# The second convolution's hand-written tile order is replaced, and its last inverse tile is split over two PSUM tiles

## The chip, the cores and the metric

The kernel runs on one core of a Trainium2 chip. The metric is the device time of one execution in microseconds (us), taken as the median of several runs. A profiled execution of the kernel before gives a trace: which instruction ran when on which engine. TensorE (PE in the profile) multiplies matrices and writes to PSUM; VectorE (DVE) and ScalarE (ACT) move results out of PSUM; SyncE (SP) issues the DMAs.

## The reference, cut to what matters

The program computes four layers on a sequence of 2048 rows with 512 channels: attention layer A, convolution layer B, then A and B again with the same weights. Each layer is preceded by a layer norm and added to its input. The change concerns only the last layer, the second B. With `u` the normalized input and `K` the convolution kernel of 2048 taps per channel, it computes

```python
Kf = rfft2(Kp)                 # K padded to 4096
Uf = rfft2(up)                 # u padded to 4096
Yf = Uf * Kf
y = irfft2(Yf)[..., :L]        # back to 2048 rows
y = y.T + u * Dskip            # the skip is folded into K before its transform
x = x + y                      # what is written out
```

## The kernel before

The convolution is done as a Fourier transform in two stages, a product, and an inverse transform in two stages, all stages as matmuls. It is class `FftB`. The channels are treated in two groups of 256 (`g` = 0 and 1), and every stage of a group is cut into 8 tiles (the last stage into 4). Each tile fills one PSUM tile `pb` of 128 x 1024 floats, which one engine then takes out of PSUM. The stages are named by one letter in an order string, which `run` walks through:

- `U` (function `f1`): first forward stage. 16 matmuls (line 756), then an eviction to `a1s` (line 745) by DVE (`UD`) or ACT (`UA`).
- `u` (function `u_f2`): second forward stage. 16 matmuls (line 763), then an eviction to `ub` by ACT (line 818). It reads all of `a1s` of its group, so the first `u` of a group needs all eight `U` evictions of it.
- `m` (function `u_mult`): product with the kernel's transform. Two DVE multiplications (line 805), into `t1` and `t2`. After each, `pump` issues three loads for a later piece of the kernel's transform on SP (lines 795 and 797), into a ring of ten.
- `y` (function `i1`): first inverse stage. 16 matmuls (lines 831 and 832), eviction to `z` (line 745) by DVE (`yD`) or ACT (`yA`). The profile names the destination `xnT` for group 0 and `z` for group 1, since group 0 reuses an older buffer. It reads all of `t1` and `t2` of its group, so the first `y` of a group needs all eight `m` of it.
- `zgt` (function `i2`): second inverse stage, tile `t` of group `g`; each tile covers four row blocks `a`. `D` means 8 matmuls (lines 847 and 848) and a DVE addition to the residual `x_sb` (line 851). `A` means four more matmuls that add the residual on PE (line 846) and a copy by ACT (line 853). `B` ("both") gives two row blocks to DVE and two to ACT. It reads all of `z` of its group. Right after each tile `store` writes it out by a DMA on SP (line 1434).

In what follows a tile is named by its letter, group and number: y13 is tile 3 of the first inverse stage of group 1. Tiles of `U`, `u`, `m` and `y` are taken in the order 00 to 07, then 10 to 17; `z` tiles carry their numbers in the order string.

The order string is written out by hand, and no scheduler moves anything: every engine executes its instructions in the string's order. What couples the engines, beside the data, is room. `ptile` deals out four PSUM tiles in rotation, so PE can start a tile only after the tile four before it has been evicted. There are three buffers for `ub`, so ACT can evict a `u` tile only after the `m` three before it is done.

PSUM tiles are tracked as a whole. In the last tile, `z13B`, DVE and ACT take halves of the same PSUM tile, and the ACT copy is made to wait for the DVE addition. The two halves are stored by two DMAs of 128 KB; all other tiles by one of 256 KB.

Of the kernel before, what the change touches and what calls it, by code (L numbers as in the profile page):

```python
# [11 lines left out]
ALU = mybir.AluOpType  # L12
# [8 lines left out]
P = 128  # L21
# [17 lines left out]
DQG = 64  # L39
# [20 lines left out]
T3 E31D x1 E30A P20 P22  # L60
"""
ORDER1 = """
UD UA UA UD UA UA UD UA UD UA UD u UD u m UA u u m UA m u u UA m UD m
u u m m m u u m u m m u u m u m m u yA yA yA m u yA yA yA yA
m yD yA yD yD yA z00D yD yA z01D yA yA z02D z03D z10D z11D z12A z13B
"""

def build_a_consts(tc, nc, cpool, tpool):
# [617 lines left out]
def build_g2(nc, tmp, p21, g2_dram, room):  # L686

    s8 = 2.0 * math.pi / 65536 * SIN_SHRINK
    own = tmp.tile([P, 2, 8 * P], I32, name="g2_i")
    gi = [own[:, 0], own[:, 1], *(room[:, (2 + h) * 16 * P:(3 + h) * 16 * P].bitcast(I32) for h in range(2))]  # L690

    def indices(h):
        for k, bias in enumerate((16384.0, 32768.0)):
            g = gi[h][:, k * 4 * P:(k + 1) * 4 * P]
            nc.gpsimd.iota(g.rearrange("p (a m) -> p a m", m=P), pattern=[[8, 4], [128, P]], base=32 * h, channel_multiplier=0)
            nc.gpsimd.tensor_scalar(g, g, p21, bias, ALU.mult, ALU.add)

    def sines(h):
        gs = room[:, h * 8 * P:(h + 1) * 8 * P]
        nc.scalar.activation(gs, low16(gi[h]), ACT.Sin, scale=s8)  # L700
        nc.sync.dma_start(g2_dram[:, :, h * 4:(h + 1) * 4, :], gs.rearrange("p (k a m) -> p k a m", k=2, a=4))

    return indices, sines


class FftB:
# [129 lines left out]
    def i2(self, g, t, eng):  # L836

        nc, x_sb = self.nc, self.x_sb
        z = self.S[g]["z"]
        dsl = slice(g * DQG * 4, (g + 1) * DQG * 4)  # L840
        p4 = self.ptile([P, 4, DQG * 4])
        n_add = {"dve": 4, "both": 2, "act": 0}[eng]
        for j in range(4):
            a = t * 4 + j
            if j >= n_add:
                nc.tensor.matmul(p4[:, j, :], lhsT=self.ident[:], rhs=x_sb[:, a, dsl], start=True, stop=False)
            nc.tensor.matmul(p4[:, j, :], lhsT=self.g2[:, 0, a, :], rhs=z[:, a, :], start=(j < n_add), stop=False)
            nc.tensor.matmul(p4[:, j, :], lhsT=self.g2[:, 1, a, :], rhs=z[:, NA + a, :], start=False, stop=True)
        if n_add:
            xr = x_sb[:, t * 4:t * 4 + n_add, dsl]  # L850
            nc.vector.tensor_tensor(xr, p4[:, 0:n_add], xr, ALU.add)
        if n_add < 4:
            nc.scalar.copy(x_sb[:, t * 4 + n_add:t * 4 + 4, dsl], p4[:, n_add:4])

    def run(self, order, u, done=lambda g, t: None, k=None, late=(), more={}):
        late, cnt = list(late), self.cnt
# [419 lines left out]
def kernel(  # L1276
# [16 lines left out]
    nc = tc.nc  # L1293
# [18 lines left out]
    u = xnT[:].rearrange("p t (b r) -> p (t b) r", r=64).rearrange("p q (a r) -> p q a r", r=4)  # L1312
# [7 lines left out]
    x_sb = xpool.tile([P, NA, D], BF16, name="x_sb")  # L1320
# [30 lines left out]
    with tc.tile_pool(name="ctmp_g2", bufs=1) as g2tmp, tc.manual_schedule(engines=MAN):  # L1351
        gx, gs = build_g2(nc, g2tmp, C["p21"], g2_dram, kp[:].rearrange("p q a r -> p (q a r)"))
# [24 lines left out]
    with tc.manual_schedule(engines=MAN):  # L1377
# [21 lines left out]
        def last(*ops):  # L1399
            def f():  # L1400
                for op, *ix in ops:
# [6 lines left out]
                     e=lambda ft: la.front_ext(3, "dve", ft))  # L1408
# [18 lines left out]
    with tc.manual_schedule(engines=MAN):  # L1427
        out_v = out.rearrange("b (p a) d -> p (b a) d", p=P)

        def store(g, t):  # L1430
            gs = slice(g * 4 * DQG, (g + 1) * 4 * DQG)
            n = 2 if (g, t) == (1, 3) else 4
            for a in range(t * 4, t * 4 + 4, n):
                nc.sync.dma_start(out_v[:, a:a + n, gs], x_sb[:, a:a + n, gs])

        fb.run(ORDER1, u, store)
    fb.c_mid.close()
# [33 lines left out]
```

## Time and profile before

| what | value |
|---|---|
| median of 4 runs | 429.02 us (428.54 to 429.66) |
| the profiled execution's own time | 429.06 us |
| its span in the trace | 427.2 us |
| granted TensorE clock over the span | 0.99 of full speed |
| DVE busy | 394.8 us, 92% of the span |
| PE busy | 353.9 us, 83% |
| ACT busy | 323.2 us, 76% |
| second convolution, first matmul to last eviction | 375.8 to 422.9 us |

The span is the time from the first to the last record of the trace; the execution's own time is 1.8 us longer. In a line of the timeline or of the chain the first number is the start in us from the beginning of the span and the second a duration in us; a bracket at the end names how long the engine had been idle before, and on whom it waited. In the table by stretch each engine has its busy time and the number of its instructions, PEclk is the TensorE clock granted (1.00 is full speed), and DMA the mean busy share of the 16 DMA engines.

### The profile page before, as it was taken

The page shows a single profiled execution, that of the slowest core. Times are in us where ns is not written, and L with a number is a line of the kernel's source. Part 1 is how long each engine was busy: PE and PEld are TensorE (multiplying, and loading weights), DVE is VectorE, ACT ScalarE, POOL GpSimd, SP SyncE. Part 2 cuts the span into 40 slices and gives each one's busy share as a digit, 9 for nine tenths or more (in the row PEclk, how much of TensorE's full clock was granted, in tenths as well). Part 3 has the DMA queues.
Part 4 walks back from the last instruction along what each step waited for, and adds up shares of the span by engine and source line. Part 5 has one row for each costly group of instructions (what it writes and reads, how often), then busy time and mean ns, then how long its engine had stood idle before and what let it go on. Part 6 is the DMA issues. An engine that isn't in the chain of part 4 may idle for free.

```text
span 427.2 us, 12737 instructions
## 1 busy us (share of the span) xinstructions
PE 353.9 (83%) x5506; PEld 264.9 (62%) x5506; DVE 394.8 (92%) x537; ACT 323.2 (76%) x554; POOL 43.9 (10%) x46
## 2 busy tenths in 40 slices
PE   3000169999999899999998899999999999997894
PEld 2000127667765687767887898555566777776793
DVE  8999999999999999996999949899999999889864
ACT  6999999986455389887999978855556568689961
POOL 3000300000598000001300000000000020000000
PEclk9999998999999899999999999999999999999999
DMA  7930732132116743572245591820141055416315
GB/s 218 392 104 12 82 78 69 33 69 58 26 41 188 243 111 99 168 308 102 77 170 188 218 329 38 258 69 2 30 111 35 2 226 219 150 52 181 118 40 161
DMA packets 62466, 54.16 MB, mean 127 GB/s; under 512 B 33893, under 2 KB 50890, under 8 KB 61130
## 3 DMA queue, kind: packets, MB, share of 16 engines
q1 hardware_dynamic: 62266, 53.22, 41.0%
q8 instruction: 43, 0.70, 0.7%
q10 hardware_dynamic: 144, 0.13, 0.1%
q14 instruction: 13, 0.11, 0.1%
HBM read 30.28 MB, written 13.24 MB: 102 GB/s over the span
## 4 chain that ended last, share of the span: by engine, by line
PE 47%; DVE 19%; ACT 10%; DMA 4%; issue 3%; SPq 2%; DVEq 0%; ACTq 0%
PE po L412 9%; DVE pav L404 5%; DVE prod L295 4%; PE pq L351 4%; PE pk L1165 4%; PE pq L424 4%; PE pp L1103 4%; PE L L302 3%; PE pp L242 3%; PE pq L185 2%; DVE t L805 2%; PE pb L831 2%; PE pb L832 2%; DVE a1s L745 2%; ACT a1s L745 2%
## 5 line engine op out<-in xcount | busy, mean ns | idle before, releaser
L404 DVE TENSOR_TENSOR pav<-attn,v_ext 128x4096 bf16<-128x4096 bf16 x32 | 73.0, 2284 | 0.3 <-DMA v_ext<-v_ext 0.3
L412 PEld LDWEIGHTS <-pav 128*128 128x128 bf16 x1024 | 59.9, 99 | 11.1 <-DVE pav L404 7.5
L295 DVE TENSOR_TENSOR prod<-qT,kT_ext 128x4096 bf16<-128x4096 bf16 x29 | 66.4, 2310 | 0.2
L412 PE MATMUL po<-ident,pav 128*128 128x128 bf16 x1024 | 63.9, 222 | 3.1 <-DVE pav L404 2.8
L1093 PE MATMUL pt<-ident,x_blk 128*128 128x128 bf16 x64 | 6.5, 252 | 43.1 <-ACT x_blk L158 43.1
L1005 DVE TENSOR_TENSOR A_t<-A_t,pow_t 128x1024 bf16<-128x1024 bf16 (+4 forms) x46 | 38.4, 879 | 0.2
L1093 PEld LDWEIGHTS <-x_blk 128*128 128x128 bf16 x64 | 5.3, 115 | 46.0 <-ACT x_blk L158 44.0
L818 ACT CAST ub<-pb 128x1024 bf16<-128x1024 f32 x32 | 32.4, 1059 | 1.3 <-DVE t L805 1.1
L353 ACT CAST v_ext<-pq 128x512 bf16<-128x512 f32 x32 | 18.8, 586 | 19.3 <-PE pq L351 18.1
L424 PE MATMUL pq<-wop,oT 128*128 128x512 bf16 x128 | 32.9, 379 | 0.0
L302 PEld LDWEIGHTS <-prod 128*128 128x128 bf16 x928 | 27.1, 96 | 8.9 <-DVE prod L295 3.2
L415 ACT CAST oT<-po 128x512 bf16<-128x512 f32 x32 | 18.6, 580 | 18.1 <-PE po L412 18.0
L1103 PE MATMUL pp<-xnT,kT_ext 128*128 128x512 bf16 x96 | 27.8, 421 | 4.7 <-ACT qT L1108 2.7
L831 PE MATMUL pb<-Wp,t 128*128 128x128 bf16 x256 | 30.2, 219 | 1.8 <-ACT ub L818 1.2
L763 PE MATMUL pb<-a1s,w_sb 128*128 128x64 bf16 x768 | 27.7, 193 | 4.8 <-ACT ub L818 3.5
L832 PE MATMUL pb<-WpJ,t 128*128 128x128 bf16 x256 | 30.0, 219 | 1.0 <-DVE t L805 1.0
L351 PE MATMUL pq<-wv,xnT 128*128 128x512 bf16 x128 | 30.7, 379 | 0.0
L745 DVE CAST a1s<-pb 128x1024 bf16<-128x1024 f32 x22 | 26.2, 1220 | 4.9 <-PE pb L756 4.8
L763 PEld LDWEIGHTS <-w_sb 128*128 128x128 bf16 x768 | 24.8, 98 | 7.5 <-issue 5.9
L302 PE MATMUL L<-ind,prod 128*128 128x8 bf16 x928 | 27.4, 166 | 1.3 <-DVE prod L295 1.1
L832 PEld LDWEIGHTS <-t 128*128 128x128 bf16 x256 | 24.9, 98 | 3.6 <-DVE t L805 1.8
L745 ACT CAST a1s<-pb 128x1024 bf16<-128x1024 f32 x26 | 25.6, 1041 | 2.0 <-PE pb L756 2.0
(227 smaller groups left out, 862.0 us busy)
## 6 DMA issues: line engine op xcount, KB each, us to landing
w_sb<-w_dram SPq DMA_DIRECT2D x8, 1024.0 KB, 7.3
w_dram<-w_zero SPq DMA_DIRECT2D x1, 4096.0 KB, 15.4
kf_ring<-kf_dram SPq DMA_DIRECT2D x13, 256.0 KB, 3.6
kf_ring<-kf_dram SPq DMA_DIRECT2D x26, 128.0 KB, 3.6
v_ext<-v_ext SPq DMA_DIRECT2D x4, 784.0 KB, 6.3
x_blk<-in_A_x_dram SPq DMA_DIRECT2D x4, 512.0 KB, 4.4
kT_ext<-in_A_wqkv_dram SPq DMA_DIRECT2D x4, 512.0 KB, 9.3
x_sb<-in_A_x_dram SPq DMA_DIRECT2D x4, 512.0 KB, 4.8
```

What stands on the lines that cost most here:

```text
L295: nc.vector.tensor_tensor(pr, self.qT[q][:, ft].unsqueeze(1).to_broadcast([P, W, 4, P]), kap, ALU.mult)
L302: self.nc.tensor.matmul(L[:, al, w, ft * 8:(ft + 1) * 8], lhsT=pr[:, w, al, :], rhs=self.c["ind8"][:], start=(ft == 0 and w == 0 and al % ...
L351: nc.tensor.matmul(pp[:], lhsT=xnT[:, dt, a * P:(a + 1) * P], rhs=wv[:, dt, :], start=(dt == 0), stop=(dt == NDT - 1))
L404: nc.vector.tensor_tensor(pv[:], attn[:, n % 4].unsqueeze(2).to_broadcast([P, W, DH, H]), vap, ALU.mult)
L412: nc.tensor.matmul(po[:, ft, :], lhsT=pvf[:, w, ft * P:(ft + 1) * P], rhs=ident[:], start=(w == 0 and ft == 0), stop=(w == W - 1), skip_gr ...
L424: nc.tensor.matmul(pw[:], lhsT=oT[:, ftp, :], rhs=self.wo[:, ftp, :], start=False, stop=(ftp == NDT - 1))
L745: (self.nc.scalar.copy if eng == "act" else self.nc.vector.tensor_copy)(dst, src)
L763: nc.tensor.matmul(p2[:, j, :], lhsT=self.w2[:, ec * EC + j, :], rhs=a1s[:, ec * EC + j, :], start=True, stop=True)
L831: nc.tensor.matmul(p3[:, j, :], lhsT=t1[:, dql, :], rhs=wp_r, start=True, stop=False)
L832: nc.tensor.matmul(p3[:, j, :], lhsT=t2[:, dql, :], rhs=wpj_r, start=False, stop=True)
L1005: return lambda: nc.vector.tensor_tensor(*args)
L1103: nc.tensor.matmul(pps[kind, b, ft][:], lhsT=la.wqk[:, dt, c:c + P], rhs=la.xnT[:, dt, b * 512:(b + 1) * 512], start=(dt == 0), stop=(dt = ...
```

## The change

The order string of the second convolution is replaced. The numbers of tiles are the same, and so is the work on PE. One `U` and one `y` tile more are evicted by DVE (8 and 5 in place of 7 and 4) and one of each fewer by ACT (8 and 11 in place of 9 and 12). The ACT tile of the last stage is `z11` in place of `z12`. The last tile, `z13B`, is made of two PSUM tiles of 128 x 512 floats, each with two row blocks: one is added by DVE, the other copied by ACT, and neither waits for the other. Its result is stored by one DMA of 256 KB, so that there are eight stores in place of nine. On all engines everything ahead of the second convolution is the same instructions in the same order.

```diff
 ORDER1 = """
-UD UA UA UD UA UA UD UA UD UA UD u UD u m UA u u m UA m u u UA m UD m
-u u m m m u u m u m m u u m u m m u yA yA yA m u yA yA yA yA
-m yD yA yD yD yA z00D yD yA z01D yA yA z02D z03D z10D z11D z12A z13B
+UD UA UD UA UD UA UD UA UD UA UD u UD u u m UA u m UD UA m u m u m
+u m UA m u m u m u m u u yD yA u m yA m m u u u m yA m yA
+yA m yD yD yA yD yA yA yA yD z01D z03D yA yA z00D z02D z12D z11A z10D z13B
 """
...
-        p4 = self.ptile([P, 4, DQG * 4])
-        n_add = {"dve": 4, "both": 2, "act": 0}[eng]
-        for j in range(4):
-            a = t * 4 + j
+        if eng == "both":
+            for h, e in enumerate(("dve", "act")):
+                self.i2_rows(z, t * 4 + 2 * h, 2, dsl, e)
+        else:
+            self.i2_rows(z, t * 4, 4, dsl, eng)
+
+    def i2_rows(self, z, a0, n, dsl, eng):
+
+        nc, x_sb = self.nc, self.x_sb
+        p4 = self.ptile([P, n, DQG * 4])
+        n_add = n if eng == "dve" else 0
+        for j in range(n):
+            a = a0 + j
...
-            xr = x_sb[:, t * 4:t * 4 + n_add, dsl]
-            nc.vector.tensor_tensor(xr, p4[:, 0:n_add], xr, ALU.add)
-        if n_add < 4:
-            nc.scalar.copy(x_sb[:, t * 4 + n_add:t * 4 + 4, dsl], p4[:, n_add:4])
+            xr = x_sb[:, a0:a0 + n, dsl]
+            nc.vector.tensor_tensor(xr, p4[:], xr, ALU.add)
+        else:
+            nc.scalar.copy(x_sb[:, a0:a0 + n, dsl], p4[:])
...
-            n = 2 if (g, t) == (1, 3) else 4
-            for a in range(t * 4, t * 4 + 4, n):
-                nc.sync.dma_start(out_v[:, a:a + n, gs], x_sb[:, a:a + n, gs])
+            ts = slice(t * 4, t * 4 + 4)
+            nc.sync.dma_start(out_v[:, ts, gs], x_sb[:, ts, gs])
```

## The prediction

> **What bounds the kernel now.** Only the second convolution changes, so I first asked the table by stretch which engine is full there.
>
> ```profile
> 380.00:384.00 4.00, 3.72 (x112) 3.24 (x107) 4.00 (x4) 3.87 (x5) 0.00 (x0) 1.00 0.02 4
> 384.00:388.00 4.00, 3.52 (x100) 3.12 (x97) 4.00 (x8) 4.00 (x5) 0.00 (x0) 1.00 0.28 69
> 402.00:406.00 4.00, 4.00 (x72) 4.00 (x72) 2.75 (x5) 4.00 (x5) 0.00 (x0) 1.00 0.00 0
> 406.00:410.00 4.00, 4.00 (x74) 4.00 (x72) 2.70 (x3) 3.21 (x4) 0.00 (x0) 1.00 0.02 4
> 414.00:418.00 4.00, 4.00 (x53) 3.74 (x51) 2.56 (x3) 1.93 (x3) 0.00 (x0) 1.00 0.32 92
> ```
>
> The columns are PE, PE's weight loads, DVE, ACT, POOL, clock, DMA share, GB/s. Up to 402 us DVE is full and PE is not; from 402 us on PE is full and DVE has about 1.3 us free in every 4. So there are two regimes. Where the second begins is seen in the timelines of ACT and DVE:
>
> ```profile
> 400.86 2.85 ACT L745 CAST xnT<-pb 128x1024 bf16<-128x1024 f32 x3
> 403.57 1.06 ACT L818 CAST ub<-pb 128x1024 bf16<-128x1024 f32 x1
> 404.48 3.82 ACT L745 CAST xnT<-pb 128x1024 bf16<-128x1024 f32 x4
> 404.66 1.29 DVE L805 TENSOR_TENSOR t<-ub,kf_ring 128x1024 bf16<-128x1024 bf16 x2 [1.21 <-ACT ub L818]
> 406.69 1.23 DVE L745 CAST xnT<-pb 128x1024 bf16<-128x1024 f32 x1 [0.73 <-PE pb L832]
> ```
>
> Between 400.86 and 408.3 us ACT evicts y00 to y06 and, after y02, the last `ub` (u17) one behind the other, a start every 0.91 us. DVE, with the last product m17 still to do, idles 1.21 us until u17 is out. PE is held by ACT too: y10 starts at 406.51, 0.05 us after ACT has emptied the PSUM tile four back (y04), and y11 and y12 likewise. From y13 on PE runs without a wait: y tiles every 0.89 us, `zD` tiles every 0.87.
>
> The end is read from the chain and the waits:
>
> ```profile
> 421.40 0.12 PE pb L848
> 421.55 0.70 DVE x_sb L851
> 422.27 0.59 ACT x_sb L853
> ACT x_sb L853 <- DVE x_sb L851: 0.8, 1, 0.8
> ```
>
> The ACT half of z13 waits for the DVE half. But computing is not all of the end:
>
> ```profile
> DMA  0007999189982999739999999999940000000000
> L1434 SPq DMA_DIRECT2D out_dram<-x_sb x9: 372/389/529, 412.5 to 422.9; - x9
> DMA to landing us min/median/max: 2.3/2.3/2.8
> ```
>
> The first line cuts 418 to 427.3 us into 40 slices: from about 422 to 425 us the DMA engines are full without a break. In the trace the last stores are issued at 421.17 (z11), 421.63 (z12), 422.27 and 422.88 (z13), and land at 423.52, 424.33, 424.81 and 425.31. Alone, 256 KB land 2.3 us after issue; in a queue each lands 0.82 us after the one before. So the end was fixed by the queue that z11's store opened: 423.52 + 0.81 + 0.98 = 425.31. The span ends 1.93 us after it.
>
> **The change part by part.** *Nothing before 375.8 us moves*; the instructions are the same.
>
> *DVE up to m17.* In the new order DVE has nine evictions before m17's end (eight `U`, and y00, which stands ahead of m12) and sixteen product pairs. Two evictions in a row start 1.14 us apart in the trace (U10, U12: 380.73, 381.87), pairs 1.205 (m11 to m13: 396.14, 397.34, 398.54). DVE starts its first eviction at 376.49 as before. If it never waits, m17 ends at 376.49 + 9 x 1.14 + 16 x 1.205 + 0.09 (the pipelined end) = 406.12. Does it wait? I carried the new order through tile by tile: each step starts at the latest of its engine being free, its operands, and its PSUM tile four back. Durations are those of the rows: 16 matmuls take 0.42 us for `U`, 0.44 for `u`, 0.84 for `y`; the eviction starts 0.26 after the last matmul's start; ACT takes 1.02, one every 0.91. The tightest places: `U` evictions on DVE have their matmuls done 0.35 us early; m07 has its `ub` 0.6 early, m10 0.9; y00 is in PSUM 1.17 early. So DVE doesn't wait once. The same walk over the old order gives every start of the trace within 0.1 us. The ring's loads don't bind: each takes SP about 1.92 us to issue, and the sixth, m17's, lands near 400, while m17 starts at 404.8.
>
> *What DVE's extra `U` and `y` cost* (2 x 1.14 us) is taken from its idle time: 1.21 + 0.73 before m17 and y07, and 0.54 ahead of U06. ACT loses two evictions, and holds PE no longer.
>
> *PE from y10.* y10 needs m17 and follows its end by 0.06: 406.18, against 406.51. From there PE has what it had: six y (0.89 to 0.90 each), z01, z03 (0.87 each), y16, y17, z00, z02, z12 (0.87 each), z11 with the residual (1.31), z10 (0.87), z13 (0.99 to its last matmul): 5.37 + 1.74 + 1.79 + 2.61 + 1.31 + 0.87 + 0.99 = 14.68. The last matmul starts at 420.86, against 421.24. PSUM room doesn't interrupt this: the nearest is y17's eviction, done 0.4 us before z12 wants it.
>
> *The last tile.* z10's addition runs from 420.07 to 421.29, z13's DVE half (0.69) behind it to 421.89, the ACT half from 421.17 to 421.76 beside it. Before, the halves ended at 422.24 and 422.86. The last eviction thus ends 0.97 us earlier, 0.59 of it from the side-by-side eviction.
>
> *Stores.* Their tiles end at about 419.6 (z12), 420.2 (z11), 421.29 (z10), 421.89 (z13); SP issues 0.05 later. Landings: z12 419.65 + 2.3 = 421.95; z11 at 422.55 by itself, but queued: 421.95 + 0.82 = 422.77; z10 421.34 + 2.3 = 423.64; z13 421.94 + 2.3 = 424.24 by itself, queued 423.64 + 0.82 = 424.46. I take the queued value, since queued stores in the trace behave so: 424.46 against 425.31, **0.85 us earlier**. Unqueued it would be 1.07. The split with the one store alone, in the old order, would bring little: the queue would still end near 424.33 + 0.82 = 425.15, 0.16 earlier. One issue fewer on SP (0.4 us) is hidden beside the DMA queue.
>
> *The clock.* The new order bunches: U17's eviction stands on ACT behind u06, and all of u10 to u13 need it. PE idles from 389.73 to 392.62, 2.9 us. That a gap costs clock shows here:
>
> ```profile
> 60.30:63.71 3.41, 1.41 (x7) 0.54 (x6) 3.41 (x5) 3.00 (x6) 0.00 (x0) 1.00 0.00 0
> 63.71:67.13 3.42, 3.28 (x14) 1.72 (x14) 3.39 (x6) 3.33 (x8) 0.00 (x0) 0.50 0.00 0
> ```
>
> A stretch with PE busy for 1.41 us, with one gap of 2.15, is followed by 3.4 us at half clock. After a gap of 2.9 I count on one such stretch in some executions. It would fall on u10 to u13: 1.86 us become 3.7, ending at 396.4 in place of 394.5; y00 then starts 1.0 late and is in PSUM at about 397.3, and DVE takes it at 397.67. Cost 0, with 0.2 to 0.4 us of cover left. With a second half-speed stretch the walk ends 0.5 to 1.2 us later than without; with a third, 1.9 to 2.8. So I take 0, and keep 0 to 1.2 for the range.
>
> The Trainium skill, "TensorE: Matmul & The Clock Gate", section "Why this matters for your kernels", warns of idle gaps above about 3 us between bursts, after which a window of idleness halves the clock; by that rule 2.9 us would just escape, while the row above shows a shorter gap followed by half speed. By either the sum is the same.
>
> **The sum.** The profiled execution took 429.06 us, 0.04 above the median. 429.06 - 0.85 = 428.2 us, 0.2% less: right at the bound of 0.2% (0.86 us), which is about what a measurement of this kernel can tell from no change.
>
> **Rivals.**
>
> *DVE loses its cover (smaller gain).* In the new order DVE has no idle time from 377.6 to 406.1, so whatever it waits comes 1:1 to the end, while before it was covered. For it: five hand-overs have only 0.35 us of slack, and y00 only 0.2 after a half-clock stretch. Against: the row durations repeat within 0.02 us. Slipping by 0.3 to 0.6 us leaves 0.25 to 0.55 of gain: 428.5 to 428.8.
>
> *The clock (slower).* If half speed lasts for more than two stretches after the gap, or a stretch falls behind y10, where PE sets the end: there 3.41 us at half speed cost 1.7, so 428.2 + 1.7 = 429.9. It decides from about 1.7 us of lost PE time on the path. Against: in the trace half speed lasted one stretch each of the two times, and from 398 us on PE is dense.
>
> *The split doesn't split.* If ACT still waited for DVE, the last eviction would end at 422.5 and land at 424.8: 428.6. The built program speaks against: the ACT copy waits for PE alone.
>
> *No queue at the end (larger gain).* With z13's store unqueued and slightly denser evictions 1.1 to 1.4 us: 427.7 to 428.0.
>
> **How the numbers follow.** The forecast has 0.58, the larger gain 0.1, a lost cover 0.2, the missing split 0.04, the clock as slower 0.06, a few mishaps of unclear sign 0.02. The forecast's own range is 428.2 with 0.3 either way, from queued to unqueued and from the scatter of medians; it lies across the bound, and I give a little over half of it, 0.37, to faster, since the queue's ends leave more room below than above. Faster: 0.37 + 0.1 + 0.01 = 0.48. Slower 0.06. The rest, 0.46, is within the bound. Range: 427.5 (a gain of 1.5) to 429.0 (a cover lost entirely).
>
> **What would show it.** In the profile after: DVE busy 4.00 in every 4 us from 380 to 404; m17 ending near 406.1 and y10 starting 0.06 later; a PE gap near 390 to 392.6; ACT's last copy starting beside DVE's last addition, near 421.2; eight stores, the last issued at 421.9. Wrong would be: a DVE wait before m17, a granted clock of 0.50 behind y10, PE waits after 406 us, or a last landing later than 424.7.

## The result, and the profile after

The kernel after takes 427.39 us (median of 42 runs, 426.96 to 428.96). The kernel before, with more runs, has a median of 428.58 us (63 runs), 0.44 us under the 429.02 of the four runs that the prediction started from. The ratio is 0.9969, 95% interval 0.9963 to 0.9975, so the change saves 1.3 us (1.1 to 1.6) by the ratio, and 1.19 us by the two medians. The forecast of 428.2 us has the right direction, but 427.39 lies 0.11 us below its range.

The profiled execution took 427.69 us, with a span of 425.9. Its table by stretch (PE, weight loads, DVE, ACT, POOL, clock, DMA share, GB/s), with the stretches of the prediction and three around PE's gap:

```profile
380.00:384.00 4.00, 3.95 (x119) 3.52 (x116) 4.00 (x4) 3.51 (x4) 0.00 (x0) 1.00 0.01 4
384.00:388.00 4.00, 3.36 (x99) 2.96 (x95) 4.00 (x7) 4.00 (x6) 0.00 (x0) 1.00 0.29 80
...
390.00:392.00 2.00, 0.00 (x0) 0.00 (x0) 2.00 (x5) 1.81 (x3) 0.00 (x0) 1.00 0.85 224
392.00:394.00 2.00, 1.64 (x32) 1.64 (x32) 2.00 (x5) 1.77 (x3) 0.00 (x0) 0.56 0.82 215
394.00:396.00 2.00, 2.00 (x43) 2.00 (x41) 2.00 (x4) 2.00 (x3) 0.00 (x0) 0.59 0.91 304
...
402.00:406.00 4.00, 3.63 (x61) 3.33 (x59) 4.00 (x8) 4.00 (x5) 0.00 (x0) 1.00 0.00 0
406.00:410.00 4.00, 4.00 (x74) 4.00 (x75) 3.25 (x3) 2.38 (x4) 0.00 (x0) 1.00 0.01 4
...
414.00:418.00 4.00, 4.00 (x47) 3.68 (x45) 3.08 (x3) 1.93 (x2) 0.00 (x0) 1.00 0.46 133
```

DVE is now full up to 406 us and PE is full from there on; ACT, which held PE between 401 and 409 us, is still full up to 406 us, but from there on it has room (2.38 of 4 us busy), and PE waits for it no longer. The gap in PE and the half-clock stretch behind it are both there (0.56 and 0.59 are means over stretches that are partly at half clock). DVE's timeline shows that neither reaches it:

```profile
376.32 8.01 DVE L745 CAST a1s<-pb 128x1024 bf16<-128x1024 f32 x7 [0.90 <-PE pb L756]
384.25 2.49 DVE L805 TENSOR_TENSOR t<-ub,kf_ring 128x1024 bf16<-128x1024 bf16 x4
386.64 1.23 DVE L745 CAST a1s<-pb 128x1024 bf16<-128x1024 f32 x1
387.78 6.11 DVE L805 TENSOR_TENSOR t<-ub,kf_ring 128x1024 bf16<-128x1024 bf16 x10
393.79 1.30 DVE L805 TENSOR_TENSOR t<-ub,w_sb 128x1024 bf16<-128x1024 bf16 x2
395.00 2.50 DVE L805 TENSOR_TENSOR t<-ub,kx 128x1024 bf16<-128x1024 bf16 x4
397.40 1.23 DVE L745 CAST xnT<-pb 128x1024 bf16<-128x1024 f32 x1
398.54 7.32 DVE L805 TENSOR_TENSOR t<-ub,kf_ring 128x1024 bf16<-128x1024 bf16 x12
405.75 2.37 DVE L745 CAST xnT<-pb 128x1024 bf16<-128x1024 f32 x2
...
419.76 1.82 DVE L860 TENSOR_TENSOR x_sb<-pb,x_sb 128x1024 bf16<-128x1024 f32 x2 [0.44 <-PE pb L857]
```

From 376.32 to 405.8 no line but the first has a bracket, so DVE waits nowhere. The last two instructions of the last line are z10 and the half of z13. ACT's timeline has the other half beside them, with no wait on DVE any more:

```profile
418.89 1.01 ACT L862 CAST x_sb<-pb 128x1024 bf16<-128x1024 f32 x1 [2.90 <-PE pb L857]
420.85 0.59 ACT L862 CAST x_sb<-pb 128x512 bf16<-128x512 f32 x1 [0.95 <-PE pb L857]
```

The stores, from the view of the DMAs between 418 and 426 us (40 slices of 0.2 us):

```profile
DMA  8999629999359999999999999999970000000003
```

and from that of the output tensor (count, duration of the issue in ns, first and last start):

```profile
L1442 SPq DMA_DIRECT2D out_dram<-x_sb x8: 372/372/394, 413.8 to 421.6; - x8
```

The DMA engines are again full up to the last landing, at 424.40. In the records of the trace the time splits thus:

| us | before | after | difference |
|---|---|---|---|
| start of DVE's first eviction | 376.49 | 376.32 | -0.17 |
| from there to the last landing | 48.86 | 48.08 | -0.78 |
| from the last landing to the end of the span (the close) | 1.89 | 1.51 | -0.38 |
| outside of the span | 1.82 | 1.78 | -0.04 |
| the execution's own time | 429.06 | 427.69 | -1.37 |

The first row lies ahead of the change, where both programs are the same. In the profiles of this study that start varies from 375.64 to 377.80, which is most of why times of single executions scatter. The second and third rows are the change: 1.16 us, which agrees with the medians' 1.19. The third was not foreseen. A landing is taken here when the last of the 16 DMA engines has reported (425.35 before, in place of the 425.31 of the prediction).

### The profile page after: what moved, and what is told of

Its sections match the earlier page's. It is cut to its first block, busy times and chain, and to the rows that moved or that the text cites. A ratio compares the mean times of both kernels' runs of the same rounds, so it can differ in the third digit from the quotient of the medians.

```text
span 425.9 us, 12735 instructions
## 1 busy us (share of the span) xinstructions
PE 355.9 (84%) x5506; PEld 266.7 (63%) x5506; DVE 396.5 (93%) x539; ACT 321.7 (76%) x552; POOL 43.9 (10%) x46
## 4 chain that ended last, share of the span: by engine, by line
PE 46%; DVE 24%; ACT 7%; issue 3%; DMA 3%; SPq 1%; DVEq 0%; ACTq 0%
PE po L412 9%; DVE t L805 6%; DVE pav L404 5%; DVE a1s L745 4%; PE pq L351 4%; PE pk L1174 4%; PE pq L424 4%; PE pp L1112 4%; PE L L302 4%; DVE prod L295 3%; PE pp L242 3%; PE pq L185 3%; PE pb L832 2%; PE pb L831 2%; DMA v_ext<-v_ext 1%
## 5 line engine op out<-in xcount | busy, mean ns | idle before, releaser
L763 PE MATMUL pb<-a1s,w_sb 128*128 128x64 bf16 x768 | 28.8, 197 | 5.2 <-ACT a1s L745 2.9
L1112 PE MATMUL pp<-xnT,kT_ext 128*128 128x512 bf16 x96 | 29.2, 437 | 3.4 <-ACT xnT L1105 1.7
L745 DVE CAST a1s<-pb 128x1024 bf16<-128x1024 f32 x23 | 27.1, 1218 | 4.3 <-PE pb L756 4.3
L763 PEld LDWEIGHTS <-w_sb 128*128 128x128 bf16 x768 | 26.1, 100 | 7.5 <-issue 5.8
```

The costliest lines, as they stand in the source:

```text
L745: (self.nc.scalar.copy if eng == "act" else self.nc.vector.tensor_copy)(dst, src)
L763: nc.tensor.matmul(p2[:, j, :], lhsT=self.w2[:, ec * EC + j, :], rhs=a1s[:, ec * EC + j, :], start=True, stop=True)
L1112: nc.tensor.matmul(pps[kind, b, ft][:], lhsT=la.wqk[:, dt, c:c + P], rhs=la.xnT[:, dt, b * 512:(b + 1) * 512], start=(dt == 0), stop=(dt = ...
```

## The experiments

What follows is compared by the two rows that belong to the change, since they repeat within 0.05 us from profile to profile, while the timed ratios of the smaller edits have intervals of 0.2% to either side, which is 0.9 us.

**Order and split apart.** `order_only` is the kernel before with the new order string and nothing else; `split_only` is the kernel after with the old order string.

> The kernel before with the new order string alone: last tile in one PSUM tile, two stores of 128 KB, nine stores in all. The tile order's share, by the walk of the prediction: last DVE half ends as in the kernel after, the ACT half 0.6 us later, last landing about 0.2 us later than in the kernel after and 0.6 earlier than in the kernel before. Theory N (the program's close, from the last landing to the end of the span, takes 1.9 us with nine stores and 1.5 with eight): close 1.9 us, so 0.6 us under the kernel before, ratio 0.9986. Rival S (the close depends on the last tile's store being one DMA of 256 KB): the same 0.9986. Rival R (the shorter close is scatter of one profile): 0.9986, and a close anywhere between 1.5 and 1.9.

> The kernel after with the old order string: the last tile in two PSUM tiles and one store of 256 KB, eight stores in all. The two evictions run side by side and end about 0.6 us earlier than in the kernel before, but the store queue hides most of it: last landing 0.1 to 0.2 us earlier. Theories N and S: the close is 0.4 us shorter as well, in all 0.5 to 0.6 us under the kernel before, ratio 0.9987. Rival R: only 0.15 us, ratio 0.9997.

Measured: `order_only` 428.46 us, ratio 0.9979 (0.9962 to 0.9995); 48.11 us from first eviction to last landing, close 1.88. `split_only` 428.20 us, ratio 0.9975 (0.9957 to 0.9994); 48.84 us and close 1.54. The closes are those of theory N. So the order brings 0.75 of the 0.78 us, and the split brings 0.02 to 0.03, where 0.1 to 0.2 had been expected of it: in the old order its evictions end at 421.69 in place of 422.86, with the same instructions ahead and a start 0.44 earlier, yet the last landing keeps its distance from the start, because the store queue fixes it. What the split and its single store do bring is the shorter close. The two parts are worth 0.75 and about 0.4 us.

**What the close goes by.** Two kernels keep the kernel after and change its stores alone:

```diff
# nine_first, and two_last with (1, 3) in place of (0, 1)
-            ts = slice(t * 4, t * 4 + 4)
-            nc.sync.dma_start(out_v[:, ts, gs], x_sb[:, ts, gs])
+            n = 2 if (g, t) == (0, 1) else 4
+            for a in range(t * 4, t * 4 + 4, n):
+                nc.sync.dma_start(out_v[:, a:a + n, gs], x_sb[:, a:a + n, gs])
```

> The kernel after, but its first store (z01) cut into two of 128 KB, so that there are nine stores and the last is still one of 256 KB. Last landing as in the kernel after. Theory N: close 1.9 us, 0.4 us over the kernel after, ratio to the kernel before 0.998. Rivals S and R: as the kernel after, ratio 0.997.

> The kernel after, but the last tile stored by two DMAs of 128 KB, nine stores. The second of the two is issued about 0.6 us after the first, last landing 0.1 to 0.3 us later than in the kernel after. Theories N and S: close 1.9 us, in all 0.5 to 0.7 us over the kernel after, ratio to the kernel before 0.9985. Rival R: 0.1 to 0.3 over the kernel after, ratio 0.9977.

Measured: `nine_first` 48.08 us and close 1.88; `two_last` 48.13 and 1.89. So the form of the last store costs next to nothing (0.05, where 0.1 to 0.3 had been expected), and with nine stores the close is 0.37 us longer wherever the ninth stands. The timed ratios, 0.9966 (0.9947 to 0.9986) and 0.9983 (0.9963 to 1.0003), are too wide to tell the theories apart; `nine_first` even lies on the rivals' side. The traces decide.

Is it the number of stores, or the number of SP's instructions? `split_load` has eight stores, and one load on SP in place of which two are issued, 55 us before the end; `seven_stores` joins two stores.

```diff
# split_load (t is 1 in the second convolution)
-        nc.sync.dma_start(self.g2[:], self.g2_dram[:])
+        for h in range(2) if t else (slice(0, 2),):
+            h = slice(h, h + 1) if t else h
+            nc.sync.dma_start(self.g2[:, h], self.g2_dram[:, h])
# seven_stores
+            if (g, t) == (0, 1):
+                return
-            ts = slice(t * 4, t * 4 + 4)
+            ts = slice(0, 8) if (g, t) == (0, 0) else slice(t * 4, t * 4 + 4)
```

> The kernel after with eight stores, but with the load of the inverse stage's matrix at the beginning of the second convolution cut into two DMAs, so that SP has one DMA more in its whole program. Theory N1 (the close goes by the stores that are still to be waited for at the end): close 1.5 us. Theory N2 (the close goes by where SP's last instructions stand in its program): close 1.9 us. The stretch from first eviction to last landing stays at 48.1 us under both.

> The kernel after with the stores of z01 and z00 joined into one of 512 KB behind z00, so that there are seven. Theory N1 (each store more to be waited for lengthens the close): close at or under 1.5 us, if it goes by steps of 0.4 about 1.1. Theory N2 (place of SP's last instructions): close 1.5 or 1.9, not less. Last landing 0 to 0.4 us later than in the kernel after, since 256 KB more are in the queue behind z00.

Measured, one execution each: `split_load` 427.75 us, 48.10 us and close 1.91; `seven_stores` 427.53 us, 48.58 and 1.48. The last store of `split_load`, first in its timeline of SP's queue (start, duration of the issue), then in its view of the DMAs (count, size, us to landing):

```profile
421.29 0.37 SPq L1444 DMA_DIRECT2D out_dram<-x_sb  x1
```

```profile
out_dram<-x_sb SPq DMA_DIRECT2D x1, 256.0 KB, 2.8
```

It lands 2.8 us after 421.29, at 424.06 to two places, and the span ends at 425.97. So the close follows SP's program, not the stores that are to be waited for: one DMA more, far away from the end, brings the longer close back. SP's records show where. Its closing instructions, in the kernel before and in the kernel after (count, duration in ns as min/median/max, first and last start):

```profile
L1466 SPq DRAIN x3: 7/7/116, 426.0 to 426.7; - x3
L1474 SPq DRAIN x3: 7/7/7, 424.8 to 425.4; - x3
```

In the kernel before, SP has passed its last wait for a landing at 425.61 and starts the first of these only at 425.98, 0.37 us later; in the kernel after the same step takes 0.05 us. The hole stands at the same point with nine stores in `order_only`, `nine_first`, `two_last` and `extra_before`; in `split_load` it stands one instruction further on; with eight or seven stores and no load more there is none.

Counting settles what these have in common. From the first record of SP in the trace, the hole is ahead of the 336th in all six profiles that have it. In the eight others the 336th record is a wait for another engine, which takes 0.44 to 0.49 us, so that a hole there would not show. And it is not the only one: in all fourteen profiles there is a hole of 0.42 to 0.44 us ahead of SP's 80th record (near 118 us) and one of 0.39 to 0.40 ahead of its 208th (near 235.5 us), that is, 128 records apart each time. 0.6 to 0.9 us after the end of each of these two, a transfer of 8192 bytes starts on the DMA queue that the profile calls "instruction". So SP stops for about 0.4 us at fixed places of its program, and an instruction more or fewer ahead of the third place decides whether it falls on a wait or beside it. That SP waits there for its own instructions is what those transfers suggest, but no run shows it.

`seven_stores` lost 0.5 us in its last landing, a little more than expected, by its one store of 512 KB.

**Is DVE the bound?** The products of m12 are done twice, in the kernel after and in the kernel before:

```diff
-        for t, k in zip(self.S[g]["t"], (kn, ks)):
+        for t, k in [*zip(self.S[g]["t"], (kn, ks))] * (2 if (self.tag, n) == (1, 12) else 1):
```

> The kernel after with the two products of m12 done twice on DVE: 1.21 us more DVE work behind y00's eviction, same results. Theory (in the new order DVE is full from its second eviction to m17, so what is added to it comes to the end in full): the stretch from DVE's first eviction to the last landing grows from 48.08 to 49.3 us. Rival (PE or ACT sets the end in the new order as it did in the old): it stays within 0.3 us of 48.1.

> The same doubling of m12's products in the kernel before. Theory (in the old order ACT's line of y00 to y06 and u17 holds PE from 401 us on, and DVE waits 1.21 us for u17): the added 1.21 us fill DVE's wait, and the stretch from DVE's first eviction to the last landing stays at 48.86 us. Rival (DVE bounds both orders up to m17): it grows by 1.2 us to 50.1.

Measured: 49.28 us and 48.86 us from first eviction to last landing, as the theory has it in both (own times 429.35 and 430.05 us, one execution each). DVE's timeline in the first and then in the second:

```profile
398.99 8.51 DVE L805 TENSOR_TENSOR t<-ub,kf_ring 128x1024 bf16<-128x1024 bf16 x14
407.41 2.36 DVE L745 CAST xnT<-pb 128x1024 bf16<-128x1024 f32 x2
```

```profile
398.33 8.61 DVE L805 TENSOR_TENSOR t<-ub,kf_ring 128x1024 bf16<-128x1024 bf16 x14
407.68 1.22 DVE L745 CAST xnT<-pb 128x1024 bf16<-128x1024 f32 x1 [0.73 <-PE pb L832]
```

In the new order the two evictions follow m17 without a bracket and everything is 1.2 us later. In the old one the doubled work fills the 1.21 us in which DVE waited for u17, and the 0.73 us wait for PE behind it is still there.

**What the half-clock stretch costs.** In `warm_gap` and `warm_new1` PE repeats the 16 matmuls of u07 in its gap, three times more:

```diff
-        for j in range(EC):
+        n = 4 if (self.tag, key, g, ec) == (1, "ua", 0, 7) else 1
+        for j in [*range(EC)] * n:
```

`warm_gap` is the kernel after with this edit.

> The kernel after, with the 16 matmuls of u07 in the second convolution issued four times over (same operands, same result) in PE's gap of 2.9 us. Theory (in the kernel after the half-clock stretch behind the gap is hidden, y00 being in PSUM before DVE comes to it): no half-clock stretch near 392 us, and yet first eviction to last landing stays at 48.1 us. Rival (the half-clock stretch costs some of the gain): under 47.9 us.

Measured: 48.07 us (own time 428.45 us, one execution), close 1.54. The table by stretch:

```profile
390.00:392.00 2.00, 1.81 (x63) 1.72 (x59) 2.00 (x4) 1.81 (x2) 0.00 (x0) 1.00 0.74 218
392.00:394.00 2.00, 0.91 (x32) 0.91 (x32) 2.00 (x5) 2.00 (x4) 0.00 (x0) 1.00 0.78 219
```

Of PE's gap of 2.67 us 1.28 us are left, the clock stays at 1.00, and nothing is gained: the half-clock stretch of the kernel after was hidden entirely. Chance shows the same: `nine_first` and `two_last` had no half-clock stretch there, `order_only` and `split_load` had one, and all four took 48.08 to 48.13 us.

**Other orders.** The prediction's way of carrying an order through gave two that should end earlier, with no y on DVE before m17 and the halved tile not last:

```diff
# order_new1
+UD UA UD UA UA UD UA UD UA UD UA UD u UD UA m u u m u u m UA m
+u u m m UA u u m u m u m m yA u u m m yA u m m u u
+yA m yA m yA yD yA yD yA yD yA z02D yD yD z00D yD yA yA z03D z01D z13B z10D z11D z12A
# order_new0
+UD UA UD UA UA UD UA UD UA UD UA UD u UD UA u m u m u m m UA u
+u u UA m u m u m u m u yA m m u m yA m u u m u m yA
+m u yA m yA yD yA yD yD yA z01D yA yD z02D yD yD yA yA z03D z00D z13B z10D z12D z11A
```

> The kernel after with another order, made by the walk of the prediction with the rows' durations: no y eviction on DVE before m17, six U evictions on DVE in place of eight, the halved tile z13 fourth from the end and z12 by ACT last. Theory (DVE's line to m17 and then PE's 14.7 us set the end): m17 ends 2.2 us earlier, y10 no longer starts with m17 but is held by the PSUM tiles, last landing 1.5 us earlier than in the kernel after; stretch from first eviction to last landing 46.6 us; close 1.5 us as with eight stores; ratio to the kernel before 0.993 to 0.994. Rival (ACT, with ten U and eight of the first eleven y, becomes the bound earlier than the walk says): 47.2 to 48.1 us, ratio 0.995 to 0.997.

> A second order from the same walk, with the same end by it (46.6 us from first eviction to last landing), but y10 follows m17 nearer and z12 on DVE, z11 on ACT are last. Theory: 46.6 us, ratio 0.993 to 0.994. Rival: 47.2 to 48.1 us, ratio 0.995 to 0.997.

Measured (`order_new1` has seven `U` evictions on DVE, not six): `order_new0` 46.82 us from first eviction to last landing, median 427.72 us, ratio 0.9974 (0.9959 to 0.9989); `order_new1` 47.71 us, median 426.68 us, ratio 0.9953 (0.9934 to 0.9972). Both ratios miss the expected 0.993 to 0.994. The traces and the medians rank them oppositely; the two intervals overlap, so the timed runs do not rank them. But the interval of `order_new0` does not reach the 0.9944 that its trace would give (48.36 us from first eviction to the end of the span, against 50.75 in the kernel before), so this one execution does not stand for the timed ones; why isn't shown. In the trace of `order_new1` the table by stretch says where 1.1 us went:

```profile
386.80:390.20 3.40, 1.62 (x45) 1.43 (x41) 3.40 (x6) 3.40 (x5) 0.00 (x0) 1.00 0.77 240
390.20:393.60 3.40, 2.49 (x48) 2.49 (x48) 3.40 (x7) 3.17 (x4) 0.00 (x0) 0.51 0.76 243
393.60:397.00 3.40, 3.40 (x52) 3.40 (x50) 3.40 (x6) 2.88 (x4) 0.00 (x0) 0.50 0.88 266
```

Two half-clock stretches in a row, and here y00 is evicted by ACT, which comes to it early: ACT waits, u13 behind y00 is late, and with it the products:

```profile
395.57 1.01 ACT L745 CAST xnT<-pb 128x1024 bf16<-128x1024 f32 x1 [0.52 <-PE pb L832]
397.53 2.50 DVE L805 TENSOR_TENSOR t<-ub,kf_ring 128x1024 bf16<-128x1024 bf16 x4 [0.50 <-ACT ub L818]
```

So I filled the gap in this order too.

> The order of order_new1, with the 16 matmuls of u07 in the second convolution issued four times over (same operands, same result), so that PE works 1.9 us in place of 0.5 in its idle gap; u07's result is still there before ACT comes to it. Theory (in order_new1's profile a half-clock stretch that followed the gap cost 1.0 us, since ACT had no cover at y00): no half-clock stretch between 388 and 398 us, stretch from first eviction to last landing 46.6 to 46.8 us, ratio to the kernel before 0.993 to 0.994. Rival (the order itself is 1.1 us slower than the walk says): 47.7 us again, ratio 0.995.

Measured: 46.75 us, close 1.54, median 427.03 us, ratio 0.9948 (0.9925 to 0.9970), and at the place of the gap

```profile
388.00:392.00 4.00, 3.11 (x96) 2.93 (x93) 4.00 (x8) 4.00 (x5) 0.00 (x0) 1.00 0.74 227
392.00:396.00 4.00, 3.02 (x78) 2.77 (x78) 4.00 (x8) 4.00 (x6) 0.00 (x0) 1.00 0.82 255
```

So with the clock held the order is as short in its profile as its walk says, to 0.15 us, and the two half-clock stretches had cost 0.96 us. What one alone would cost in this order isn't shown. By its trace this kernel is 1.30 us shorter than the kernel after (48.29 against 49.59 from first eviction to the end of the span). By its ratio it beats the kernel before; its interval overlaps that of the kernel after by a little.

The Trainium skill, "TensorE: Matmul & The Clock Gate", section "Part 1: The HAM clock gate (the "warmup" mystery)", says that the activity window is free-running and doesn't reset when a kernel starts. The profiles fit this: of the seven with the new order and PE's gap unfilled, five (392.2, 393.4, 392.4, 392.9 and 391.8 us) had a half-clock stretch behind it and two had none. The limit of about 3 us that the prediction quoted from that page is too high for these runs, since the gap takes 2.67 us in the records of all seven, and 2.12 in `order_new1`.

## Why the prediction was right or wrong

*DVE up to m17: right.* Counted from DVE's first eviction, m17 was to end at 29.63 us and ended at 29.53; y10 was to start at 29.69 and started at 29.59. That DVE waits nowhere is in the timeline, that it has become the bound is shown by the doubled products.

*PE from y10: right.* 14.68 us to the last matmul's start were forecast, 14.64 passed. ACT held nothing.

*The last tile: right.* DVE's half was to end at 45.40 after the first eviction and did at 45.27, and ACT's 0.15 before it.

*Stores: right, a little too good.* Forecast 0.85 us, measured 0.78. The term that was mis-sized is the spacing of queued stores of 256 KB: I took 0.82 us; in the trace after the queued ones land 0.94 (z11) and 0.86 (z13) after the one before. Taken by the last DMA engine as here, z11 and z12 already landed 0.90 apart in the trace before. That the split alone would bring 0.16 by the stores was too much as well: it is 0.02.

*The clock: right, and shown.* PE's gap was put at 2.9 us and took 2.67. The half-clock stretch came where it was put, and cost nothing.

*The end of the span: wrong.* "The span ends 1.93 us after it" was carried over as a constant, as if nothing in the change could touch it, and "One issue fewer on SP (0.4 us) is hidden beside the DMA queue" priced the ninth store by its issue alone. The close became 0.38 us shorter, because, with two instructions fewer on SP, its stop of 0.37 us no longer shows among the closing ones. With it the gain is 1.16 us (0.78 and 0.38), where 0.85 was forecast, and faster by more than 0.2% is a clear answer, where I had called it even.

*The time that the sum started from: off.* 429.06 us was one execution of a kernel whose median over 63 runs is 428.58, and the four runs at hand had their median as high, at 429.02. From 428.58 the sum's own 0.85 us give 427.7; with the measured 0.78 and the missed 0.38 it is 427.4. Of the 0.82 us between the sum (428.21) and the median, 0.48 are this and 0.31 the larger gain. The miss needed both: with a close as long as before the median would have been 427.77, and from a kernel at 429.06 it would have been 427.87, both inside the range. The range was made from what could go wrong inside the convolution, and held neither the scatter of a median of four nor a change in how the program closes.

*The rivals.* A lost cover and a split that doesn't split did not happen. A gain of the size of the larger one (1.1 to 1.4 us) happened, but not by its mechanism: the last store was queued, and the gain came behind it. The slower case needed more than two half-clock stretches; at most two in a row were seen, in another order.

## What to carry to other kernels

Where two engines meet at a point in an order written by hand, add up each one's work to that point from the rows: the line that has no wait is the bound, and a walk through the order with the rows' durations gave here every stage within 0.15 us (two further orders ended 0.15 and 0.2 us behind their walk, one of them only with the clock held). When an engine's idle time is used up, look for what its cover was hiding: one half-clock stretch cost nothing where a full DVE came late to the result, and two in a row cost 1 us where an ACT with time to spare came early. Evicting the last tile faster is worth little while a queue of stores fixes the end, and a DMA taken out of SP's program can be worth more by the program's close than by its transfer, if one of SP's stops stands at the close.

## What the runs showed of the hardware that was not expected

The time from the last landing to the end of the span takes two values, 1.48 to 1.54 us and 1.88 to 1.91 us, over fourteen profiles. The longer one has a hole of 0.36 to 0.37 us in SP's records close to the program's end, and a single DMA more in SP's program, 55 us before, makes it show there. Like holes of 0.39 to 0.44 us stand 128 and 256 of SP's records ahead of that place in every profile. Half clock can last for two stretches in a row (390.2 to 397.0 us in `order_new1`) with PE at work in both.
